# Raw query weights for every token block, a pair product on VectorE, and a new spread of the fill products in a fused attention and Fourier kernel

## The chip, the core and the metric

The kernel runs on one core of a Trainium2 chip. The metric is device time in microseconds (us) of one execution, smaller is better; it is given as the median of several runs. The engines are TensorE (PE in the profile; PEld is its weight load), VectorE (DVE), ScalarE (ACT), GpSimd (POOL) and SyncE (SP), which here issues every DMA, in its own order.

## What is computed

Two independent sublayers whose results are put side by side: multi-query attention A (32 heads of width 32, one key head and one value head) and a Fourier mixing sublayer B, on 2048 tokens of width 1024, all in float32.

```python
def _A_ref(x, wq, wk, wv, wo):                    # x: (1, 2048, 1024), wq: (1024, 1024), wk, wv: (1024, 32)
    q = (x @ wq).reshape(B, S, H, Dh).transpose(0, 2, 1, 3)
    k = x @ wk
    v = x @ wv
    scores = jnp.einsum("bhqd,bkd->bhqk", q, k) * (Dh ** -0.5)
    p = _softmax(scores, axis=-1)
    o = jnp.einsum("bhqk,bkd->bhqd", p, v)
    return o.transpose(0, 2, 1, 3).reshape(B, S, H * Dh) @ wo

def _B_ref(x, dft_seq_re, dft_seq_im, dft_hid_re, dft_hid_im):
    a = jnp.einsum("bsd,ed->bse", x, dft_hid_re)
    b = jnp.einsum("bsd,ed->bse", x, dft_hid_im)
    return jnp.einsum("ts,bse->bte", dft_seq_re, a) - jnp.einsum("ts,bse->bte", dft_seq_im, b)

return jnp.concatenate([a, b], axis=-1)
```

## The kernel before

**Two streams of matmuls, woven into one order.** Everything is written out in Python as one static program; every engine executes its instructions in the order in which they are written (the class `Ordered`, whose line 66 is therefore the line of nearly every row of the profile; tiles tell the groups apart). The first stream is attention proper. The second is the *fill*: all large matrix products (projections, both Fourier stages, the output projection), cut into *groups* that each accumulate 12 or 24 matmuls in a PSUM bank `psb`. `take(n)` writes the next n fill products; `pos["fill"]` counts them.

**Precision.** A large product of float32 matrices is made of three fast matmuls: both operands are split into a high part (a cast to float32r) and a low part (value minus high part), and `product` issues hi x hi, hi x lo and lo x hi (rows `psb<-rh,mh`, `psb<-rl,mh`, `psb<-rh,ml`). `m` are left operands (weights in `mh`, `ml`), `r` right ones (`rh`, `rl`). The cast and the subtraction are done by ACT and DVE for the first `START` = 120 products and by POOL after that (`cast`, `lo`).

**The lines that prepare operands.** `ML` handles left items, `RL` right ones. Each item passes four steps: load, combine, high part, low part. `ML` may start them 52, 36, 27 and 21 products before the item is due, and at most three raw items are staged at once (`NM0`). An item with `pre` skips load and combination: `fetch` moves its two finished parts from DRAM straight into `mh` and `ml` at the third step. An item with `save` has both parts stored to DRAM after they are made. `store` writes its DMA nine products later (`BEHIND`). `force` brings an item through all steps at once where the product needs it.

**Query groups.** `q_group(b, g, xs)` projects token block b (512 tokens, four blocks) for head group g (four heads, eight groups). Its left operand is the weight slice of head group g in two items of 256 KB. For a g that appears for the first time (block 0) they are loaded raw, split and saved in `wq_d`; in the blocks 1 to 3 the saved parts are fetched. The post step scales the result into `qh`, `ql` (parts; `ql` has one buffer) and stores both to DRAM.

**Attention.** A *unit* is a pair (b, g); there are 32 of them, with 32 steps each. `open_unit` reads a unit's query parts into the stacked operand `qst`, six steps before its scores begin. `scores(s)` makes two matmuls into `pss` (two buffers) and a negated maximum on DVE into `nm`; `row_sums` follows with the exponential on ACT and its row sums. 44 steps later (`SU + LEAD`), `expo(n)` makes the transposed scores in `pst` (one buffer) and their exponential `p`, and every eighth step `pv` multiplies by the values. Between scores and `expo` the log-sum work of the unit runs at certain steps (the table `LSE`): offsets of the two halves (`lse_1`, DVE), their exponential (`lse_1b`, ACT), the product of that with the row sums (`lse_1c`, POOL), the sum and reciprocal (`lse_2`, DVE), a transpose on PE and a copy `mt` (`lse_3`), and the DMAs that write the offsets into rows 96 and 97 of `qst` (`lse_4`). The unit's first `expo` reads these rows.

**The weave.** A prologue takes 120 products, opens unit 0, takes 66 more, and runs 44 score steps with seven products each. The main loop has 1024 steps: `score_step`, `expo`, at every eighth step `pv` and else `level(n)`, which takes as many products as bring the count to a goal that rises evenly over all steps. In the last 44 steps there are no scores left. At the end, `LAST` = 24 products are left over for the tail, and 192 products of the last block, added 12 steps before the end, follow. `aside`, called ahead of a transpose or `pv`, takes up to five products more where a group is just begun or nearly done.

Of the kernel before, what the change touches and what calls it, by code (L numbers as in the profile page):

```python
# [8 lines left out]
F32 = mybir.dt.float32  # L9
F32R = mybir.dt.float32r  # L10
AF = mybir.ActivationFunctionType
ALU = mybir.AluOpType
AX = mybir.AxisListType
# [3 lines left out]
P = 128  # L17
# [5 lines left out]
NG = 8  # L23
NQ = 4
NC = 16
# [62 lines left out]
def tile_kernel(ctx: ExitStack, tc, xT, wq, wkv, wo, xbT, wT, cT, out):  # L88
    nc = tc.nc
    te = Ordered(tc, nc.tensor)  # L90
    act = Ordered(tc, nc.scalar)
    dve = Ordered(tc, nc.vector)
    gp = Ordered(tc, nc.gpsimd)
# [3 lines left out]
    def pool(stack, name, bufs, **kw):  # L97
        kw.setdefault("reuse_waits", "tile")
        return stack.enter_context(tc.tile_pool(name=name, bufs=bufs, **kw))

    dram = ctx.enter_context(tc.tile_pool(name="dram", bufs=1, space=DRAM))
# [2 lines left out]
    oh_d = [dram.tile([NG, P, W], F32, name=f"oh_{b}") for b in range(NQ)]  # L104
    ol_d = [dram.tile([NG, P, W], F32, name=f"ol_{b}") for b in range(NQ)]
    r_d = [dram.tile([NC, P], F32, name=f"r_{u}") for u in range(NQ * NG)]
    wq_d = [[[dram.tile([P, 4, P], F32, name=f"wq_{g}_{q}_{a}") for a in range(2)] for q in range(2)] for g in range(NG)]
    xr_d = [dram.tile([P, 4, P], F32, name=f"xr_{k}") for k in range(8)]
    wr_d = [[dram.tile([P, W], F32, name=f"wr_{n}_{c}") for c in range(4)] for n in range(2)]
    u_d = {(n, k): [dram.tile([P, W], F32, name=f"{k}_{n}_{s}") for s in range(8)] for n in range(2) for k in ("t", "u2", "u3", "u4")}  # L110
# [3 lines left out]
    ident = keep.tile([P, P], F32, name="ident")  # L114
# [17 lines left out]
    op = pool(ctx, "op", 2, side="right")  # L132
    hp = pool(ctx, "hp", 1, side="right")

    def move(q, to, of):
        q.dma_start(to.bitcast(F32), of.bitcast(F32))
# [35 lines left out]
    pos = {"fill": 0, "s": 0}  # L172
# [145 lines left out]
    def store(to, of, key=None):  # L318
        def go():
            move(sp, to, of)  # L320
            if key:
                ready.add(key)
        soon(go)
# [4 lines left out]
    def bank(name, open_=False):  # L328

        b = 1 - cur["bank"] if cur["bank"] is not None else int(used[1] < used[0])  # L330
        cur["at"] += 1
        used[b] = cur["at"]
        if open_:
            cur["bank"] = b
        return ps_b[b].tile([P, W], F32, name=name)
# [16 lines left out]
    def take(n):  # L352
        for _ in range(n):
            if cur["group"] >= len(groups):
                return
            g = groups[cur["group"]]
            j = pos["fill"] - g.at
            if j == 0:
                cur["ps"] = bank("psb", True)
            if j % 3 == 0:  # L360
                RL.force(g.right[j // 3])
            if j % 12 == 0:
                ML.force(g.left[j // 12])
            product(g, cur["ps"], j)
            pos["fill"] += 1
            if j == g.n - 1:
                cur["group"] += 1
                assert all(hasattr(it, "done") for it in g.ys)
                g.post(cur["ps"])
                cur["at"] += 1  # L370
                used[cur["bank"]] = cur["at"]
                cur["bank"] = None
                if g.ys:
                    at(pos["fill"] + 2 * BEHIND, lambda n=len(g.ys): yused.__setitem__(0, yused[0] + n))
            pump()
            run_later()

    def aside():

        if cur["group"] >= len(groups):  # L380
            return
        g = groups[cur["group"]]
        j = pos["fill"] - g.at
        if 0 < j < 6:
            take(6 - j)
        elif j > g.n - 6:
            take(g.n - j)
# [29 lines left out]
        return Group(wkv_items, xs, kv_post(b), rows=2 * DH)  # L417

    ready = set()
    seen_w = set()  # L420

    def q_group(b, g, xs):
        if g in seen_w:
            left = [Item(None, pre=lambda q=q: wq_d[g][q]) for q in range(2)]
        else:
            seen_w.add(g)
            left = [Item([(lambda q=q: wq[g, :, q * 4:(q + 1) * 4, :], 1)], save=wq_d[g][q]) for q in range(2)]

        def post(ps):
            qh = op.tile([P, W], F32R, name="qh")  # L430
            ql = op.tile([P, W], F32R, name="ql", bufs=1)
            if pos["fill"] <= START:
                act.activation(qh, ps, AF.Copy, scale=scale)
            else:
                dve.tensor_scalar_mul(qh, ps, scale)
            dve.scalar_tensor_tensor(ql, ps, scale, qh.bitcast(F32), op0=ALU.mult, op1=ALU.subtract)
            store(qh_d[b][g], qh)
            store(ql_d[b][g], ql, ("q", b, g))
        return Group(left, xs, post)
# [126 lines left out]
    def x_groups(b, kv, q):  # L566
        xs = x_set(b)
        return ([kv_group(b, xs)] if kv else []) + ([q_group(b, g, xs) for g in range(NG)] if q else [])
# [12 lines left out]
    sm = pool(ctx, "sm", 2)  # L581
# [3 lines left out]
    SU = 32  # L585
    LEAD = 12
    total = SU * len(units)
    qst, nm, ls, lse, pt, ov, rb, pend = ({} for _ in range(8))
    ends = []

    def open_unit(u):
        b, g = units[u]
        assert ("q", b, g) in ready
        q = qsp.tile([P, 4, W], F32R, name="qst")
        gp.memset(q[96:P].bitcast(F32), 0.0)
        for r, src in enumerate((qh_d, ql_d, qh_d)):
            move(sp, q[r * DH:(r + 1) * DH], src[b][g].rearrange("(h d) c -> d h c", d=DH))
        qst[u] = q
        nm[u] = sm.tile([P, 6, NC], F32, name="nm")
        ls[u] = sm.tile([P, 2, NC], F32, name="ls")  # L600

    def scores(s):
        u, r = divmod(s, SU)
# [9 lines left out]
    def row_sums(s):  # L613
        if s not in pend:
            return
        ps = pend.pop(s)
        u, r = divmod(s, SU)
        i, j = divmod(r, 2)
        act.activation(ps, ps, AF.Exp, bias=nm[u][:, j, i:i + 1], accum_out=ls[u][:, j, i:i + 1])

    def over(rows):
        return rows.rearrange("p a c -> p c a")

    def lse_1(u):
        z = nm[u]
        d = sm.tile([P, 2, NC], F32, name="md")
        dve.tensor_reduce(z[:, 2], over(z[:, :2]), axis=AX.X, op=ALU.min, negate=True)
        for j in range(2):
            dve.tensor_reduce(d[:, j], over(z[:, j::2 - j][:, :2]), axis=AX.X, op=ALU.add, negate=True)
        lse[u] = d  # L630

    def lse_1b(u):
        act.activation(lse[u], lse[u], AF.Exp)

    def lse_1c(u):
        gp.tensor_mul(lse[u], lse[u], ls[u])

    def lse_2(u):
        z, d = nm[u], lse[u]
        l = sm.tile([P, NC], F32, name="l")  # L640
        dve.tensor_reduce(z[:, 3].bitcast(F32R), over(z[:, :2]), axis=AX.X, op=ALU.min)
        dve.tensor_reduce(z[:, 4], over(z[:, 2:4]), axis=AX.X, op=ALU.add, negate=True)
        dve.tensor_reduce(l, over(d), axis=AX.X, op=ALU.add)
        dve.reciprocal(z[:, 5], l)

    def lse_3(u):
        aside()
        pm = bank("psb")
        te.transpose(pm[:3 * NC, :P], nm[u][:, 3:].rearrange("p a b -> p (a b)"), ident)
        mt = sm.tile([3 * NC, P], F32, name="mt")  # L650
        dve.tensor_copy(mt, pm[:3 * NC, :P])
        cur["at"] += 1
        lse[u] = mt
# [54 lines left out]
    def score_step(s):  # L708

        if s < total:  # L710
            u, r = divmod(s, SU)
            if r == SU - 6 and u + 1 < len(units):
                open_unit(u + 1)
            scores(s)
        row_sums(s - 1)
        u, e = divmod(s - SU, SU)
        if 0 <= u < len(units):
            for f in LSE.get(e, ()):
                f(u)

    LSE = {1: (lse_1,), 2: (lse_1b,), 3: (lse_1c,), 6: (lse_2,), 7: (lse_3,), 9: (lse_4,)}

    room = [(lambda t=t, k=k: t[:, k]) for t in [pp.tile([P, 2, W], F32, name="p") for _ in range(9)] for k in range(2)]
    room += [(lambda t=t: t) for t in [hp.tile([P, W], F32, name=f"h{k}") for k in range(8)]]
# [5 lines left out]
    pump()  # L730
    take(START)
    open_unit(0)
    take(66)
    for s in range(SU + LEAD):
# [3 lines left out]
    PRO = pos["fill"]  # L738
    FILL = end[0]
    LAST = 24  # L740


    def level(n):
        k, r = divmod(n, 8)
        if r == 0:
            return
        goal = PRO + (FILL - PRO - LAST) * (k + 1) * 8 // total
        left = goal - pos["fill"]
        take(left - left * (7 - r) // (8 - r))

    for n in range(total):
        u, r = divmod(n, SU)
        if n == total - 12:
            w1 = wo_set(1)
            add([o_group(NQ - 1, t, e, ws) for e, ws in ((0, w0), (1, w1)) for t in range(4)])
        score_step(n + SU + LEAD)
        if ends:
            ends.pop(0)()
        expo(n)
        if r == 16:  # L760
            inverse(u)
        if r % 8 == 0 and n:
            pv(*divmod(n // 8 - 1, 4))
        level(n)
# [29 lines left out]
    for t, g in enumerate(last[4:]):  # L794
        ps = ps_b[t % 2].tile([P, W], F32, name="psb")
# [41 lines left out]
```

## Time and profile before

| | before |
|---|---|
| median of 3 runs | 2813.98 us (2813.29 to 2816.73) |
| the profiled execution | 2816.89 us |
| span of its trace, first to last instruction | 2815.0 us |
| mean granted TensorE clock | 0.997 |
| moved by DMA | 480.84 MB, 171 GB/s on average |

In a row of the profile, the first number of a busy entry is time in us, x is a count, and "out<-in" names the tile written and those read. In a timeline a row begins with its start and its duration; in brackets stands how long the engine had been idle before, and what ended that. The matmuls of PE are pipelined: their durations overlap, and the distance between two starts is what one costs.

### The profile page before, as it was taken

What the parts mean: (1) busy time and instruction counts of PE and PEld (TensorE: products, weight loads), DVE (VectorE), ACT (ScalarE), POOL (GpSimd) and SP (SyncE); (2) the same over time, 40 slices, a digit from 0 to 9 for tenths busy, and PEclk for the clock granted to TensorE, in tenths of its full rate; (3) what the DMA queues carried; (4) which work ended last, traced back from release to release, by engine and by line L of the source; (5) the groups of instructions that cost most, each with busy time, mean ns of one, the idle gap of its engine ahead of it and who ended that gap; (6) DMA issues with size and microseconds to landing.
All of it is one profiled execution on the core that took longest, in us unless ns stands there. A gap on an engine that the chain in (4) does not pass through costs nothing.

```text
span 2815.0 us, 40144 instructions
## 1 busy us (share of the span) xinstructions
PE 2776.0 (99%) x13904; PEld 1935.7 (69%) x13904; DVE 1612.9 (57%) x1800; ACT 2182.6 (78%) x3151; POOL 1569.4 (56%) x1558
## 2 busy tenths in 40 slices
PE   7999999999999999999999999989999999999999
PEld 5776676767667676767666767666767676766656
DVE  5766666666666665555555555545555555555411
ACT  4578887888878788888888888878888888888740
POOL 2422233665545448767785676887888875721110
PEclk9999999999999999999999999999999999999999
DMA  8865435675576555554463454564554642545345
GB/s 292 299 199 163 156 109 169 225 231 188 195 243 211 166 178 167 152 155 142 140 191 105 127 172 122 184 198 138 183 176 146 187 139 98 159 145 145 122 143 172
DMA packets 315723, 480.84 MB, mean 171 GB/s; under 512 B 33408, under 2 KB 98432, under 8 KB 315520
## 3 DMA queue, kind: packets, MB, share of 16 engines
q1 hardware_dynamic: 315520, 478.28, 54.3%
q8 instruction: 110, 1.80, 0.3%
q14 instruction: 93, 0.76, 0.1%
HBM read 364.12 MB, written 112.98 MB: 169 GB/s over the span
## 4 chain that ended last, share of the span: by engine, by line
PE 93%; DMA 2%; POOL 1%; issue 1%; DVE 1%; SPq 1%; ACT 1%; POOLq 0%; DVEq 0%; ACTq 0%
PE psb L66 59%; PE pss L66 18%; PE pst L66 17%; DMA r<-s 1%; DMA ql<-ql 1%; SPq L66 1%; POOL ml L66 0%; DMA r<-in_xT_dram 0%; DVE nm L66 0%; POOL mh L66 0%; POOL m L66 0%; DMA wq<-mh 0%; POOL rl L66 0%; POOL rh L66 0%; POOL y L66 0%
## 5 line engine op out<-in xcount | busy, mean ns | idle before, releaser
L66 DVE TENSOR_REDUCE nm<-pss 128x1 f32<-128x1024 f32 x1024 | 1252.2, 1223 | 611.7 <-PE pss L66 610.9
L66 ACT ACTIVATE p<-pst 128x1024 f32<-128x1024 f32 x1024 | 1052.0, 1027 | 481.0 <-PE pst L66 478.9
L66 ACT ACTIVATE pss<-pss,nm 128x1024 f32<-128x1024 f32 x1024 | 1112.7, 1087 | 72.7 <-DVE nm L66 71.6
L66 PE MATMUL psb<-rh,mh 128*128 128x512 f32 (+1 forms) x1852 | 732.0, 395 | 17.9 <-ACT rh L66 8.7
L66 PE MATMUL psb<-rh,ml 128*128 128x512 f32 (+1 forms) x1852 | 731.9, 395 | 1.4 <-POOL ml L66 1.4
L66 PE MATMUL psb<-rl,mh 128*128 128x512 f32 (+1 forms) x1852 | 730.1, 394 | 0.3 <-DVE rl L66 0.3
L66 PE MATMUL pst<-qst,kst 128*128 128x512 f32 x2048 | 654.3, 400 | 5.6 <-DMA qst<-mt 4.7
L66 PE MATMUL pss<-kst,qst 128*128 128x512 f32 x2048 | 655.8, 401 | 3.2 <-ACT pss L66 3.2
L66 PEld LDWEIGHTS pss<-kst,qst 128*128 128x128 f32 x2048 | 375.6, 188 | 185.3 <-issue 100.5
L66 PE MATMUL psb<-p,v 128*32 128x512 f32 x4096 | 466.6, 596 | 0.0
L66 PEld LDWEIGHTS pst<-qst,kst 128*128 128x128 f32 x2048 | 375.8, 188 | 116.6 <-ACT p L66 26.6
L66 PEld LDWEIGHTS psb<-rh,mh 128*128 128x128 f32 (+1 forms) x1852 | 347.6, 188 | 105.8 <-ACT rh L66 10.0
L66 PEld LDWEIGHTS psb<-rh,ml 128*128 128x128 f32 (+1 forms) x1852 | 347.8, 188 | 86.0 <-POOL ml L66 2.8
L66 PEld LDWEIGHTS psb<-rl,mh 128*128 128x128 f32 (+1 forms) x1852 | 347.4, 188 | 84.2 <-DVE rl L66 1.4
L66 POOL TENSOR_TENSOR ml<-m,mh 128x512 fp32r<-128x512 f32 x292 | 376.5, 1289 | 49.2 <-ACT mh L66 43.6
L66 PEld LDWEIGHTS psb<-p,v 128*32 128x32 f32 x4096 | 120.5, 110 | 276.3 <-issue 266.0
L66 POOL TENSOR_TENSOR r<-r,r 128x512 f32<-128x512 f32 x112 | 144.3, 1288 | 269.7 <-DMA r<-in_wT_dram 135.0
L66 POOL CAST rh<-r 128x512 fp32r<-128x512 f32 x214 | 131.2, 613 | 275.0 <-PE psb L66 110.1
L66 POOL TENSOR_TENSOR rl<-r,rh 128x512 fp32r<-128x512 f32 x214 | 276.0, 1290 | 5.5
L66 POOL TENSOR_TENSOR m<-m,m 128x512 f32<-128x512 f32 x192 | 247.6, 1290 | 24.4 <-DMA m<-in_xbT_dram 18.8
L66 DVE TENSOR_TENSOR ov<-ov,psb 128x512 f32<-128x512 f32 x96 | 66.0, 687 | 314.2 <-PE psb L66 314.2
L66 POOL CAST mh<-m 128x512 fp32r<-128x512 f32 x291 | 178.0, 612 | 91.4 <-PE psb L66 76.0
(69 smaller groups left out, 926.5 us busy)
## 6 DMA issues: line engine op xcount, KB each, us to landing
m<-in_cT_dram SPq DMA_DIRECT2D x384, 256.0 KB, 3.8
r<-s SPq DMA_DIRECT2D x192, 256.0 KB, 4.4
y<-y SPq DMA_DIRECT2D x96, 256.0 KB, 4.6
r<-in_wT_dram SPq DMA_DIRECT2D x80, 256.0 KB, 3.6
m<-in_xbT_dram SPq DMA_DIRECT2D x80, 256.0 KB, 4.2
y<-u SPq DMA_DIRECT2D x80, 256.0 KB, 2.9
qst<-qh SPq DMA_DIRECT2D x64, 256.0 KB, 5.7
s<-y SPq DMA_DIRECT2D x64, 256.0 KB, 2.9
```

Source lines behind the costliest of these rows:

```text
L66: return lambda *a, **k: self.tc.keep_in_program_order(f(*a, **k))
```

## The change

Three edits. (1) No query weight part is kept in DRAM: `wq_d` is gone, and each of the four token blocks loads each weight item raw and splits it. (2) The product of the exponentiated offsets with the row sums moves from POOL (`lse_1c`) to DVE, as two reductions with a multiplication in `lse_2`; for that, the row sums and offsets become rows 6 to 9 of `nm`, and the table `LSE` has the steps 1, 2, 4, 6, 8 in place of 1, 2, 3, 6, 7, 9. (3) The goal of `level` no longer rises evenly: each step past `QUIET` = 980 has one product more, and all steps share the rest.

```diff
--- before.py
+++ after.py
@@ -104,7 +104,6 @@
     oh_d = [dram.tile([NG, P, W], F32, name=f"oh_{b}") for b in range(NQ)]
     ol_d = [dram.tile([NG, P, W], F32, name=f"ol_{b}") for b in range(NQ)]
     r_d = [dram.tile([NC, P], F32, name=f"r_{u}") for u in range(NQ * NG)]
-    wq_d = [[[dram.tile([P, 4, P], F32, name=f"wq_{g}_{q}_{a}") for a in range(2)] for q in range(2)] for g in range(NG)]
     xr_d = [dram.tile([P, 4, P], F32, name=f"xr_{k}") for k in range(8)]
     wr_d = [[dram.tile([P, W], F32, name=f"wr_{n}_{c}") for c in range(4)] for n in range(2)]
     u_d = {(n, k): [dram.tile([P, W], F32, name=f"{k}_{n}_{s}") for s in range(8)] for n in range(2) for k in ("t", "u2", "u3", "u4")}
@@ -417,14 +416,9 @@
         return Group(wkv_items, xs, kv_post(b), rows=2 * DH)
 
     ready = set()
-    seen_w = set()
 
     def q_group(b, g, xs):
-        if g in seen_w:
-            left = [Item(None, pre=lambda q=q: wq_d[g][q]) for q in range(2)]
-        else:
-            seen_w.add(g)
-            left = [Item([(lambda q=q: wq[g, :, q * 4:(q + 1) * 4, :], 1)], save=wq_d[g][q]) for q in range(2)]
+        left = [Item([(lambda q=q: wq[g, :, q * 4:(q + 1) * 4, :], 1)]) for q in range(2)]
 
         def post(ps):
             qh = op.tile([P, W], F32R, name="qh")
@@ -585,7 +579,7 @@
     SU = 32
     LEAD = 12
     total = SU * len(units)
-    qst, nm, ls, lse, pt, ov, rb, pend = ({} for _ in range(8))
+    qst, nm, lse, pt, ov, rb, pend = ({} for _ in range(7))
     ends = []
 
     def open_unit(u):
@@ -596,8 +590,7 @@
         for r, src in enumerate((qh_d, ql_d, qh_d)):
             move(sp, q[r * DH:(r + 1) * DH], src[b][g].rearrange("(h d) c -> d h c", d=DH))
         qst[u] = q
-        nm[u] = sm.tile([P, 6, NC], F32, name="nm")
-        ls[u] = sm.tile([P, 2, NC], F32, name="ls")
+        nm[u] = sm.tile([P, 10, NC], F32, name="nm")
 
     def scores(s):
         u, r = divmod(s, SU)
@@ -616,28 +609,26 @@
         ps = pend.pop(s)
         u, r = divmod(s, SU)
         i, j = divmod(r, 2)
-        act.activation(ps, ps, AF.Exp, bias=nm[u][:, j, i:i + 1], accum_out=ls[u][:, j, i:i + 1])
+        act.activation(ps, ps, AF.Exp, bias=nm[u][:, j, i:i + 1], accum_out=nm[u][:, 8 + j, i:i + 1])
 
     def over(rows):
         return rows.rearrange("p a c -> p c a")
 
     def lse_1(u):
         z = nm[u]
-        d = sm.tile([P, 2, NC], F32, name="md")
         dve.tensor_reduce(z[:, 2], over(z[:, :2]), axis=AX.X, op=ALU.min, negate=True)
         for j in range(2):
-            dve.tensor_reduce(d[:, j], over(z[:, j::2 - j][:, :2]), axis=AX.X, op=ALU.add, negate=True)
-        lse[u] = d
+            dve.tensor_reduce(z[:, 6 + j], over(z[:, j::2 - j][:, :2]), axis=AX.X, op=ALU.add, negate=True)
 
     def lse_1b(u):
-        act.activation(lse[u], lse[u], AF.Exp)
-
-    def lse_1c(u):
-        gp.tensor_mul(lse[u], lse[u], ls[u])
+        act.activation(nm[u][:, 6:8], nm[u][:, 6:8], AF.Exp)
 
     def lse_2(u):
-        z, d = nm[u], lse[u]
+        z = nm[u]
+        d = sm.tile([P, 2, NC], F32, name="md")
         l = sm.tile([P, NC], F32, name="l")
+        for j in range(2):
+            dve.tensor_reduce(d[:, j], over(z[:, 6 + j::2][:, :2]), axis=AX.X, op=ALU.mult)
         dve.tensor_reduce(z[:, 3].bitcast(F32R), over(z[:, :2]), axis=AX.X, op=ALU.min)
         dve.tensor_reduce(z[:, 4], over(z[:, 2:4]), axis=AX.X, op=ALU.add, negate=True)
         dve.tensor_reduce(l, over(d), axis=AX.X, op=ALU.add)
@@ -646,7 +637,7 @@
     def lse_3(u):
         aside()
         pm = bank("psb")
-        te.transpose(pm[:3 * NC, :P], nm[u][:, 3:].rearrange("p a b -> p (a b)"), ident)
+        te.transpose(pm[:3 * NC, :P], nm[u][:, 3:6].rearrange("p a b -> p (a b)"), ident)
         mt = sm.tile([3 * NC, P], F32, name="mt")
         dve.tensor_copy(mt, pm[:3 * NC, :P])
         cur["at"] += 1
@@ -718,7 +709,7 @@
             for f in LSE.get(e, ()):
                 f(u)
 
-    LSE = {1: (lse_1,), 2: (lse_1b,), 3: (lse_1c,), 6: (lse_2,), 7: (lse_3,), 9: (lse_4,)}
+    LSE = {1: (lse_1,), 2: (lse_1b,), 4: (lse_2,), 6: (lse_3,), 8: (lse_4,)}
 
     room = [(lambda t=t, k=k: t[:, k]) for t in [pp.tile([P, 2, W], F32, name="p") for _ in range(9)] for k in range(2)]
     room += [(lambda t=t: t) for t in [hp.tile([P, W], F32, name=f"h{k}") for k in range(8)]]
@@ -740,12 +731,18 @@
     LAST = 24
 
 
+    QUIET = total - SU - LEAD
+    MORE = 1
+
+    def goal(n):
+        return PRO + (FILL - PRO - LAST - MORE * (total - QUIET)) * n // total + MORE * max(n - QUIET, 0)
+
+
     def level(n):
         k, r = divmod(n, 8)
         if r == 0:
             return
-        goal = PRO + (FILL - PRO - LAST) * (k + 1) * 8 // total
-        left = goal - pos["fill"]
+        left = goal((k + 1) * 8) - pos["fill"]
         take(left - left * (7 - r) // (8 - r))
 
     for n in range(total):
```

## The prediction

> **What bounds the kernel now.** I read the page first: which engine is full, and whether its clock is whole.
>
> ```profile
> PE 2776.0 (99%) x13904; PEld 1935.7 (69%) x13904; DVE 1612.9 (57%) x1800; ACT 2182.6 (78%) x3151; POOL 1569.4 (56%) x1558
> PE 93%; DMA 2%; POOL 1%; issue 1%; DVE 1%; SPq 1%; ACT 1%; POOLq 0%; DVEq 0%; ACTq 0%
> ```
>
> TensorE (PE) is occupied 2776.0 of 2815.0 us and is 93% of the chain that ended last. The diff neither adds nor removes a matmul, so time can come only from three places: the 39 us in which PE stands, stretches in which it is busy but slow, and stretches in which another engine dictates the step while PE's occupied time hides it. Next I read the table by stretches for where the first kind lies.
>
> ```profile
> 60.00:80.00 20.00, 15.15 (x50) 11.17 (x51) 7.68 (x8) 4.81 (x8) 15.84 (x19) 0.83 1.04 386
> 80.00:100.00 20.00, 20.00 (x88) 16.21 (x87) 15.00 (x17) 11.84 (x19) 11.39 (x12) 1.00 0.89 310
> 300.00:400.00 100.00, 100.00 (x513) 69.62 (x512) 63.57 (x75) 82.62 (x121) 31.27 (x34) 1.00 0.41 128
> 2720.00:2740.00 20.00, 19.93 (x106) 11.51 (x109) 2.07 (x3) 9.26 (x10) 6.49 (x8) 1.00 0.48 142
> ```
>
> Columns: stretch, length, busy time of PE, weight loads, DVE, ACT, POOL, then granted clock, DMA share, GB/s. From 60 to 80 us PE loses 4.85 us, the granted clock is 0.83, and the DMA engines are full (share 1.04). From 80 on PE is gapless, with POOL at 11.39 of 20 us. At 2720 the page shows a full PE; the instructions below show otherwise.
>
> **Part A: the weight parts no longer stored.** I followed PE's timeline through the bad stretch. "psb" matmuls are fill products, "pss" the first scores.
>
> ```profile
> 54.25 0.47 PE L66 MATMUL psb<-rh,mh 128*128 128x512 f32 x1
> 57.57 0.40 PE L66 MATMUL psb<-rh,ml 128*128 128x512 f32 x1
> 60.40 0.50 PE L66 MATMUL psb<-rh,mh 128*128 128x512 f32 x1 [2.43 <-POOL mh L66]
> 62.34 0.63 PE L66 MATMUL psb<-rh,mh 128*128 128x512 f32 x1
> 62.77 0.63 PE L66 MATMUL psb<-rl,mh 128*128 128x512 f32 x1
> 63.62 0.90 PE L66 MATMUL pss<-kst,qst 128*128 128x512 f32 x2
> 66.72 0.47 PE L66 MATMUL psb<-rh,mh 128*128 128x512 f32 x1 [0.82 <-DVE ql L66]
> 74.54 1.22 PE L66 MATMUL pss<-kst,qst 128*128 128x512 f32 x2 [3.18 <-ACT pss L66]
> 80.33 0.62 PE L66 MATMUL pss<-kst,qst 128*128 128x512 f32 x2
> ...
> 80.95 1.62 PE psb L66 x7
> 83.04 1.62 PE psb L66 x7
> ```
>
> The last two lines are of the chain of waits: seven products take 1.62 us, 0.2317 us each, and a prologue step of seven products and two score matmuls takes 83.04 - 80.95 = 2.09 us. The product at 54.25 is number 168 (seven groups of 24). Scores begin after number 186, and the pair at 80.33 is the sixth, five steps later. Unhindered that is 18 x 0.2317 + 5 x 2.09 = 14.6 us; it took 26.08. So 11.5 us are lost here. The waits shown are 6.4 of them. After each long wait the products also start 0.43 apart (62.34, 62.77) instead of 0.23.
>
> [...]
>
> Who is late? DMA issues from 50 to 80 us, SP's and POOL's queues, and DVE's:
>
> ```profile
> DMA packets 5695, 10.38 MB, mean 346 GB/s; under 512 B 633, under 2 KB 633, under 8 KB 5694
> m<-in_wq_dram SPq DMA_DIRECT2D x9, 256.0 KB, 5.1
> wq<-mh SPq DMA_DIRECT2D x8, 256.0 KB, 5.2
> wq<-ml SPq DMA_DIRECT2D x8, 256.0 KB, 5.2
> ...
> 47.93 0.39 SPq L66 DMA_DIRECT2D ql<-ql  x1
> 52.72 0.32 SPq L66 DMA_DIRECT2D qst<-qh  x1
> 54.21 0.38 SPq L66 DMA_DIRECT2D m<-in_wq_dram  x1
> ...
> 59.74 0.61 POOL L66 CAST mh<-m 128x512 fp32r<-128x512 f32 x1 [4.40 <-DMA m<-in_wq_dram]
> 65.88 0.69 DVE L66 SCALAR_TENSOR_TENSOR ql<-psb,qh 128x512 fp32r<-128x512 f32 x1 [10.91 <-DMA ql<-ql]
> ```
>
> Two chains. The load issued at 54.21 lands only at 59.74, so POOL's cast and PE are late. And ql has one buffer: its next writer on DVE waits 10.91 us for the previous store, with the score reductions behind it on DVE, and so the exponentials (ACT) and the score banks PE waits for (3.18). In both the DMA engines are full, and 16 transfers of 256 KB, 4.2 of the stretch's 10.4 MB, are the wq stores that the change deletes. Each also takes SP about half a microsecond of issue. One delay stays: SP stands from 48.3 to 52.72 for the first query store to land, as the load of qst must follow it. With the traffic down to 60% I expect landing nearer 3 us than 5, the load issued at 52 and landed at 56, just ahead of its need at 57.8. Bounds: nothing (the traffic was not the cause) to 11.5. I take 8.5, near the upper end since both chains end in a transfer that shared full DMA engines.
>
> **Part B: raw weights in blocks 1 to 3.** 96 fetches of parts (2 per item) become 48 raw loads, and POOL gains 48 casts and 48 subtractions:
>
> ```profile
> L66 POOL TENSOR_TENSOR ml<-m,mh 128x512 fp32r<-128x512 f32 x292 | 376.5, 1289 | 49.2 <-ACT mh L66 43.6 <-PE psb L66 1.7
> L66 POOL CAST mh<-m 128x512 fp32r<-128x512 f32 x291 | 178.0, 612 | 91.4 <-PE psb L66 76.0 <-DMA m<-in_xbT_dram 8.7 <-DMA m<-in_wq_dram 5.3
> L66 POOL TENSOR_TENSOR md<-md,ls 128x32 f32<-128x32 f32 x32 | 8.1, 253 | 160.8 <-ACT md L66 160.0 <-PE psb L66 0.8
> L66 DVE TENSOR_REDUCE md<-nm 128x16 f32<-128x32 f32 x64 | 9.0, 183 | 1.1
> ```
>
> 48 x (1.289 + 0.612) = 91 us of POOL. A group needs two weight items and about one item of the next x set, 3 x 1.9 = 5.7 us. It lasts 24/7 steps of 2.09, 7.2 us, in the prologue; in the main loop, with 4.84 products a step (part D), 24/4.84 steps of at least 2.09, over 10.4 us. So POOL is at 80%, then below 55%; in block 0 it carries that load already and PE is gapless from 80 to 100. Parts are made 21 products ahead, and DMA at 0.41 has room. Cost: nothing, hidden under PE's products; if the cover fails, part A's wait comes back (a rival below).
>
> **Part C: the pair product.** POOL loses 32 products of 253 ns; DVE gains 64 reductions, priced by the nearest row at 183 ns: 11.7 us, in DVE's 43% idle time. What matters is the order. Now DVE's sum waits in order for POOL, the reductions and a bank's release behind it. With two ACT and DVE instructions instead, the exponential was issued two steps earlier, ahead of the exponentials that free the score bank DVE reads just before. So no new wait. The transpose comes two steps behind its input instead of one, and the move of the offsets into qst one step earlier (8, not 9). The worst unit:
>
> ```profile
> 1857.03 0.19 DVE L66 TENSOR_REDUCE l<-md 128x16 f32<-128x32 f32 x1 [2.12 <-POOL md L66]
> 1858.50 0.67 DVE L66 TENSOR_TENSOR h<-h,psb 128x512 f32<-128x512 f32 x1
> ...
> 1857.56 0.29 PE L66 MATMUL psb<-ident,nm 128*48 128x128 f32 x1 [1.66 <-DVE nm L66]
> 1859.32 0.51 PE L66 MATMUL psb<-rh,mh 128*128 128x512 f32 x1 [1.00 <-POOL r L66]
> 1876.03 1.19 PE L66 MATMUL pst<-qst,kst 128*128 128x512 f32 x2 [4.72 <-DMA qst<-mt]
> ...
> 1869.83 0.81 SPq L66 DMA_DIRECT2D m<-in_cT_dram  x2
> 1871.69 1.71 SPq L66 DMA_DIRECT2D qst<-mt  x2
> ```
>
> POOL late, so DVE late, so the transpose (1.66) and the bank that h's addition empties (1.00; the page names POOL, but this fits). Then qst's move stands in SP's queue behind loads until 1871.69. 7.4 us of waits, and slow products after them. The first 2.7 should go; of the 4.72, an earlier issue by one step (over 2 us) should save most, about 3; slow products 0.8 more. I take 6.5. Bounds: -2 (SP's order changes, and another unit's move is late by a step) to 9 (all waits with their slow products).
>
> **Part D: one more product in the last 44 steps.** Now every main step takes (5472 - 497 - 24)/1024 = 4.84 products: the groups before the final eight hold 36 x 24 + 112 x 12 + 112 x 24 + 24 x 24 = 5472, the prologue uses 120 + 66 + 44 x 7 and about 3 that close a group, and 24 are kept for last. So 44 x 980/1024 = 42 products leave the first 980 steps, where PE sets the pace: 42 x 0.2317 = 9.7 us saved. They reappear at the end:
>
> ```profile
> 2710.55 0.73 PE L66 MATMUL pst<-qst,kst 128*128 128x512 f32 x2
> 2712.46 0.73 PE L66 MATMUL pst<-qst,kst 128*128 128x512 f32 x2
> 2709.47 1.03 ACT L66 ACTIVATE p<-pst 128x1024 f32<-128x1024 f32 x1 [0.88 <-PE pst L66]
> ```
>
> Scores are over here, and each step is a ring through the single pst buffer: matmul, 1.03 us of exponential, matmul. It takes 1.91 us with five products (2710.55 to 2712.46), although these seven matmuls need only 7 x 0.2317 = 1.62. A sixth product makes 1.85 and is free; a seventh makes 9 x 0.2317 = 2.09, so costs 0.18. Following the goal formula through these steps gives about 13 steps with seven (2.3 us), and five more products beside the p,v matmuls (1.1). Net 9.7 - 3.4 = 6.3 us. Bounds: 0 (the first 980 steps gain nothing, ACT setting them) to 9.7.
>
> **Sum.** 8.5 + 0 + 6.5 + 6.3 = 21.3 us. The profiled execution took 2816.9 us, the runs' median is 2814.0. By the one the new time is 2795.6, by the other 2792.7. I predict midway, 2794, that is 2815.4 less the gain.
>
> **Rivals.** (1) *The waits move.* SP's stand for the first query store is still there and its load still late, so A gives 4; in stage 2 POOL, near full, makes another qst move late, so C gives 0. 2815.4 - 10.3 = 2805. For it: SP's 4.4 us stand. Against: a third of the traffic is gone. (2) *Everything recovered*: A 11.5, C 9, D 7.5: 28 us, 2787. Against: SP's stand at 48.3 us remains. (3) *Slower: raw loads of blocks 1 to 3 come late*, because SP, which waits for POOL to free staging buffers, issues them behind other waits. The pattern is that of 60.40: the six products from 57.8 should have ended at 59.2, the score came at 63.62, so 4.4 us per miss. From five misses of 48 it eats the gain; with eight, 2815.4 - 21.3 + 35.2 = 2829. For: block 0 had such a miss in its 14 items. Against: DMA at 0.41 and POOL at 31.27 of 100 us there. (4) *Nothing comes of it*: a burst of loads replaces the stores, A 4, and ACT, whose two exponentials fill a five-product step, limits the first 980 steps, C and D 0: 2811.
>
> **How the numbers follow.** Forecast 0.60, with its own range 2788 to 2801; rivals in order 0.18, 0.10, 0.07, 0.05. A measurement here can tell about 0.2%, 5.6 us, from no change. The forecast, (1) and (2) are faster by more: 0.88; (4) is the same: 0.05; (3) slower: 0.07. The range runs from 2785 (below rival 2) to 2809 (past rival 1); it leaves out (3) and (4), and some edge.
>
> **What would show it.** Right: no PE wait over 1 us from 50 to 80, clock 1.00 and DMA well under 0.9 there, the sixth score pair near 72 us; POOL some 80 us busier, all before 360; no wait for md or qst<-mt over 1 us near 1860; the first 980 main steps about 1 us shorter per 100, and the last 44 filled with six or seven products at 1.91 to 2.09. Wrong: PE waits for POOL mh between 100 and 360 us, or the stretch from the first main step to the last score shortens by less than 5 us beyond the waits named.

## The result and the profile after

| | before | after |
|---|---|---|
| median | 2813.87 us (2813.29 to 2816.73, 4 runs) | 2797.23 us (2795.68 to 2801.67, 4 runs) |
| the profiled execution, and its span | 2816.89, 2815.0 us | 2797.06, 2795.1 us |

The ratio of after to before is 0.9941, 95% interval 0.9924 to 0.9959: 16.6 us faster by the medians, 19.8 by the profiled executions. To see where, I cut both traces at the starts of ACT's exponentials of the transposed scores (`p<-pst`, one per main step): the first one, the 981st, the last.

| stretch | before, us | after, us | difference | predicted |
|---|---|---|---|---|
| start to first main step | 164.74 | 156.08 | -8.66 | -8.5 (A) |
| first 980 main steps | 2494.81 | 2480.24 | -14.57 | -9.7 (D) and -6.5 (C) |
| the last steps, to the 1024th | 94.65 | 97.94 | +3.29 | +3.4 (D) |
| tail | 60.8 | 60.8 | 0 | 0 |

The page's engine line and the table by stretches of the changed kernel (columns as before):

```profile
PE 2764.2 (99%) x13904; PEld 1931.4 (69%) x13904; DVE 1621.7 (58%) x1864; ACT 2181.3 (78%) x3151; POOL 1650.5 (59%) x1622
...
40.00:60.00 20.00, 20.00 (x91) 16.27 (x90) 6.87 (x11) 2.38 (x4) 13.52 (x15) 1.00 0.81 259
60.00:80.00 20.00, 18.42 (x81) 14.62 (x80) 14.04 (x16) 10.50 (x17) 15.34 (x18) 1.00 0.66 222
80.00:100.00 20.00, 20.00 (x87) 16.06 (x86) 14.90 (x16) 11.14 (x20) 15.74 (x18) 1.00 0.46 154
300.00:400.00 100.00, 100.00 (x511) 68.94 (x510) 62.29 (x72) 82.84 (x121) 36.45 (x38) 1.00 0.34 109
```

From 60 to 80 us the DMA share fell from 1.04 to 0.66, the clock is whole, and PE loses 1.6 us where it lost 4.85. POOL is 81 us busier in all, and PE is gapless from 80 to 100 and from 300 to 400 as before.

The start in SP's queue and on PE, then the bad unit near 1850 us on PE, DVE and SP:

```profile
44.83 0.32 SPq L66 DMA_DIRECT2D ql<-ql  x1
46.84 0.32 SPq L66 DMA_DIRECT2D qst<-qh  x1
48.74 0.35 SPq L66 DMA_DIRECT2D m<-in_wq_dram  x1
...
66.23 0.73 PE L66 MATMUL pss<-kst,qst 128*128 128x512 f32 x2 [1.58 <-ACT pss L66]
70.49 0.62 PE L66 MATMUL pss<-kst,qst 128*128 128x512 f32 x2
142.83 0.47 PE L66 MATMUL psb<-rh,mh 128*128 128x512 f32 x1 [1.69 <-DVE ql L66]
1855.61 0.70 PE L66 MATMUL pst<-qst,kst 128*128 128x512 f32 x2 [3.56 <-DMA qst<-mt]
...
1839.91 0.27 DVE L66 COPY mt<-psb 48x128 f32<-48x128 f32 x1
...
1848.74 0.81 SPq L66 DMA_DIRECT2D m<-in_cT_dram  x2
1850.60 1.15 SPq L66 DMA_DIRECT2D qst<-mt  x2
```

SP's stand for the first query store shrank from 4.4 us to 1.7 (45.15 to 46.84), and the sixth score pair comes at 70.49 in place of 80.33. In the bad unit (unit 20, counted from 0) the wait for the pair product is gone, but `mt` is ready at 1840.2 and its move is issued only at 1850.60, behind loads; the loads themselves came late, at 1842.76 and 1848.74, right behind POOL's subtractions `ml<-m,mh`, which ended at 1842.73 and 1848.71. PE stands 3.56 us where it stood 4.72.

Of the last steps, three rows with a distance of one step each, and two from further on, all from PE's timeline:

```profile
2665.55 0.74 PE L66 MATMUL pst<-qst,kst 128*128 128x512 f32 x2
2667.73 0.62 PE L66 MATMUL pst<-qst,kst 128*128 128x512 f32 x2
2669.82 0.62 PE L66 MATMUL pst<-qst,kst 128*128 128x512 f32 x2
...
2692.45 0.67 PE L66 MATMUL pst<-qst,kst 128*128 128x512 f32 x2
2694.35 0.67 PE L66 MATMUL pst<-qst,kst 128*128 128x512 f32 x2
```

The first of these steps takes 2.18 us, the second 2.09, both with seven products; the third, with six, takes 1.90. Of the last 44 steps 13 have seven, as forecast.

### The profile page after: what moved, and what is told of

It reads as the page before. It is cut to its first block, busy times and chain, and to the rows that moved or that the text cites. A ratio compares the mean times of both kernels' runs of the same rounds, so it can differ in the third digit from the quotient of the medians.

```text
span 2795.1 us, 40153 instructions
## 1 busy us (share of the span) xinstructions
PE 2764.2 (99%) x13904; PEld 1931.4 (69%) x13904; DVE 1621.7 (58%) x1864; ACT 2181.3 (78%) x3151; POOL 1650.5 (59%) x1622
## 4 chain that ended last, share of the span: by engine, by line
PE 93%; DMA 2%; POOL 1%; issue 1%; DVE 1%; ACT 1%; SPq 1%; POOLq 0%; ACTq 0%; DVEq 0%
PE psb L66 59%; PE pss L66 18%; PE pst L66 16%; DMA r<-s 1%; SPq L66 1%; POOL ml L66 0%; DMA p<-in_xT_dram 0%; DVE nm L66 0%; DMA r<-in_xT_dram 0%; ACT pss L66 0%; DVE y L66 0%; ACT p L66 0%; POOL mh L66 0%; ACT rh L66 0%; DMA ql<-ql 0%
## 5 line engine op out<-in xcount | busy, mean ns | idle before, releaser
L66 POOL TENSOR_TENSOR ml<-m,mh 128x512 fp32r<-128x512 f32 x340 | 438.7, 1290 | 48.3 <-ACT mh L66 40.6
L66 POOL CAST mh<-m 128x512 fp32r<-128x512 f32 x339 | 207.4, 612 | 169.0 <-PE psb L66 149.8
```

Source lines behind the costliest of these rows:

```text
L66: return lambda *a, **k: self.tc.keep_in_program_order(f(*a, **k))
```

## The experiments

Open were whether the parts add up, whether the stores cause the loss at the start, whether VectorE or the earlier places helped in part C, and why the wait for `qst<-mt` stayed. The table has, for each profiled execution, the time to the first main step, the first 980 main steps, the rest to the 1024th, and the lengths of unit 15 and unit 20 (32 steps each, counted from 0, from a unit's first exponential to the next unit's); then the median and the ratio to before, with its interval, from runs of before on the same chip beside it. The changed kernel was timed apart from the others: the median of before was 2813.87 us beside it, and 2814.83 to 2815.21 beside them, so differences of medians between its row and another hold to about 1.3 us.

| run | start | first 980 | last | unit 15 | unit 20 | median | ratio (95%) |
|---|---|---|---|---|---|---|---|
| before | 164.74 | 2494.81 | 94.65 | 81.95 | 90.85 | 2813.87 | |
| after | 156.08 | 2480.24 | 97.94 | 80.51 | 86.09 | 2797.23 | 0.9941 (0.9924, 0.9959) |
| spread_only | 163.92 | 2487.66 | 98.50 | 86.13 | 87.91 | 2814.42 | 0.9996 (0.9988, 1.0005) |
| raw_only | 154.87 | 2492.71 | 94.66 | 80.60 | 89.78 | 2806.90 | 0.9969 (0.9957, 0.9981) |
| pair_only | 166.64 | 2486.47 | 94.63 | 80.58 | 82.50 | 2808.97 | 0.9977 (0.9968, 0.9986) |
| after_stores | 166.09 | 2480.85 | 97.96 | 80.52 | 87.43 | 2808.38 | 0.9974 (0.9964, 0.9985) |
| raw_pair | 156.06 | 2484.69 | 94.70 | 80.58 | 81.93 | 2801.61 | 0.9951 (0.9937, 0.9964) |
| late_lse | 158.05 | 2493.69 | 98.46 | 86.44 | 87.91 | 2810.27 | 0.9985 (0.9977, 0.9994) |
| pool_early | 158.26 | 2481.81 | 97.95 | 80.83 | 88.59 | 2800.64 | 0.9953 (0.9940, 0.9965) |
| mt_act | 157.96 | 2535.98 | 97.94 | 85.49 | 95.76 | 2854.57 | 1.0144 (1.0130, 1.0158) |
| more2 | 156.09 | 2468.55 | 105.26 | 80.06 | 84.36 | 2799.43 | 0.9944 (0.9931, 0.9956) |
| ql_y | 154.09 | 2478.95 | 97.90 | 80.52 | 86.76 | 2796.70 | 0.9941 (0.9927, 0.9954) |
| early_lse | 156.47 | 2477.04 | 98.79 | 80.88 | 82.82 | 2793.75 | 0.9923 (0.9911, 0.9936) |
| early_ql | 153.26 | 2475.86 | 98.78 | 80.84 | 82.49 | 2789.84 | 0.9910 (0.9897, 0.9924) |

**The three parts alone.** `spread_only` is the kernel before with the new `goal` alone.

> The kernel before with only the new goal of the fill products. Theory (the sum by parts): the first 980 main steps lose 42 products of 0.2317 us, about 9.7 us, and the last 44 steps grow by about 3.3, so 6 to 6.5 us faster than before, ratio near 0.9977; the start and the wait near 1870 us stay. Rival (ACT limits the first 980 steps): these steps do not get shorter, so 3 us slower.

By the medians it gives nothing that can be measured, against the 6 to 6.5 us expected. The rival's cause falls all the same, as the first 980 steps are 7.15 us shorter. The trace says where most of the gain went: the last steps cost 3.85 us more as expected, all units but 15 and 20 together are 8.4 us shorter (7.15, plus 4.18 lost in unit 15, less 2.94 gained in unit 20), but unit 15, undisturbed before, has a new stall:

```profile
1460.47 1.19 PE L66 MATMUL pst<-qst,kst 128*128 128x512 f32 x2 [4.20 <-DMA qst<-mt]
...
1449.72 0.33 SPq L66 DMA_DIRECT2D m<-in_cT_dram  x1
1455.28 0.33 SPq L66 DMA_DIRECT2D m<-in_cT_dram  x1
1456.66 1.15 SPq L66 DMA_DIRECT2D qst<-mt  x2
```

Moving products shifts the weave's phase against the units, and with it where SP's loads stand ahead of the small move: here the move is issued 10.0 us after `mt` is ready, behind two loads that had waited for POOL. The 8.4 us come near 42 times 0.23; that the saving stays was wrong.

`raw_only` is the kernel before with the raw loads alone (the three lines of `q_group` and no `wq_d`).

> The kernel before with only the raw weight loads. Theory: the time to the first main step falls from 164.7 to about 156 us and nothing else moves, so 8.7 us faster, ratio near 0.9969. Rival (the raw loads and POOL's 91 us in blocks 1 to 3 cost time later): the main steps grow by over 2 us and the gain is under 6.5.

The start is 9.9 us shorter, the main steps did not grow: 2.1 us shorter, 1.35 and 1.07 of it in the units 15 and 20, and no other differs by over 0.15. POOL's 91 us cost nothing that shows. The theory holds.

`pair_only` is the kernel before with the new log-sum work alone.

> The kernel before with only the pair product on VectorE and the earlier steps of the log-sum work. Theory: the wait for the pair product in the worst unit (2.7 us) goes, the late move into qst stays or shrinks a little, so the main steps are 3 to 5 us shorter, ratio 0.998 to 0.999. Rival (the unit's stall has another cause, such as the weave's phase, and the gain there came from the moved fill products): under 1.5 us, or none.

```profile
1868.18 0.70 PE L66 MATMUL pst<-qst,kst 128*128 128x512 f32 x2 [1.26 <-DMA qst<-mt]
```

Its main steps are 8.3 us shorter, more than the theory's 3 to 5, and all of it in unit 20 (90.85 to 82.50); the gains and losses of the others cancel. The wait for the move, 4.72 us before, is 1.26 here. The rival falls.

By the ratios the three parts alone save 0.31%, 0.23% and 0.04%, in sum 0.58% or 16.3 us; together they save 0.59%, 16.6 us. So they add up, as far as intervals of about 0.1% on each can tell.

**The stores.** `after_stores` is the changed kernel that also stores block 0's parts, which nothing reads (the line that makes `wq_d`, as before, is left out here):

```diff
-        left = [Item([(lambda q=q: wq[g, :, q * 4:(q + 1) * 4, :], 1)]) for q in range(2)]
+        left = [Item([(lambda q=q: wq[g, :, q * 4:(q + 1) * 4, :], 1)], save=wq_d[g][q] if b == 0 else None) for q in range(2)]
```

> The changed kernel, which also stores the weight parts of block 0 to DRAM as before did, and never reads them. Theory (the stores fill the DMA engines and SP's queue at the start): the first main step comes 8 to 9 us later, near 165 us, and the whole is 8 to 9 us slower than the changed kernel. Rival (the gain came from the later blocks, which no longer fetch parts): under 3 us slower.

```profile
59.66 0.50 PE L66 MATMUL psb<-rh,mh 128*128 128x512 f32 x1 [1.49 <-POOL mh L66]
66.36 0.47 PE L66 MATMUL psb<-rh,mh 128*128 128x512 f32 x1 [0.89 <-DVE ql L66]
74.92 1.22 PE L66 MATMUL pss<-kst,qst 128*128 128x512 f32 x2 [3.91 <-ACT pss L66]
```

The three waits of before are back at their places, though of other lengths, the start is 10.0 us longer, the main steps are the changed kernel's to 0.6 us. The stores alone made the loss; the fetches of the later blocks made none.

**The spread in company.** `raw_pair` is the changed kernel with `MORE = 0`, `more2` with `MORE = 2`.

> The changed kernel with the old, even goal of the fill products. Theory (42 products of 0.2317 us leave the first 980 steps, and stalls that depend on the weave's phase take part of it back): the last 44 steps are 3.3 us shorter than the changed kernel's 97.9, the first 980 are 6 to 10 us longer, of which units other than 20 carry 9 to 10 and unit 20 itself gets shorter; 3 to 6 us slower in all. Rival (the spread is worth nothing here either, as alone): within 1.5 us.

The first 980 steps are 4.45 us longer, and 8.6 without unit 20, which is itself 4.2 shorter; the last steps are 3.2 shorter. The sizes come near the theory's (8.6 where 9 to 10 stood, 3.2 where 3.3 stood), but the first 980 steps as a whole stay under its 6 to 10. By the trace the spread is worth 1.2 us, which is the rival's case; by the medians 4.4, which is the theory's; the profiled execution is the lowest of its five, and the two intervals overlap. So what the spread is worth in company stays open between 1 and 4 us.

> The changed kernel with two more fill products per step in the last 44 steps in place of one. Theory (the sixth product is free there, the seventh costs 0.18 us, the eighth its full 0.23): the first 980 steps are 9.7 us shorter but for stalls that move, the last 44 longer by 8 to 10, so within 2 us of the changed kernel. Rival (the last steps have more room than the ring of 1.91 us shows): 4 us or more faster.

First steps 11.7 us shorter, last ones 7.3 longer, where 9.7 and 8 to 10 were expected. By the traces that is 4.4 us faster, as the rival had it, but this profiled execution, 2792.83 us, is the lowest of five by 4.9; by the medians the kernel is 2.2 us slower, and the ratio is that of the changed kernel. So no gain is shown. In the ring, a step with eight products takes 2.31 us for 2.09 with seven: the room is used up, as expected.

**Engine or place.** `late_lse` is the changed kernel with the pair product on VectorE, but the old places; `pool_early` has the new places, but the product on POOL. The edit of `late_lse`:

```diff
-    LSE = {1: (lse_1,), 2: (lse_1b,), 4: (lse_2,), 6: (lse_3,), 8: (lse_4,)}
+    LSE = {1: (lse_1,), 2: (lse_1b,), 6: (lse_2,), 7: (lse_3,), 9: (lse_4,)}
```

> The changed kernel with the pair product on VectorE, but with the log-sum steps at the places of before (sum at 6, transpose at 7, moves at 9). Theory A (the engine is what helped, the places little): the wait for DVE nm ahead of a transpose stays gone, and unit 20 is within 1.5 us of the changed kernel's 86.1. Theory B (the earlier issue of the moves is what helped): the wait for qst<-mt grows by about 2 us, and a wait of over 1 us comes up in some other unit of the second Fourier stage, 2 to 5 us slower in all.

13 us slower by the medians, and in the trace the first 980 steps are 13.45 us longer. Theory A falls: unit 20 is 1.8 us longer than the changed kernel's. Theory B is right in kind, as another unit has a wait of 4.54 us for the move, but not in size, and the wait in unit 20 did not grow (3.34 us). The grouped rows of the transpose's weight load, before, after, and here with the wait:

```profile
L66 PEld LDWEIGHTS psb<-ident,nm 128*48 128x48 f32 x32 | 3.3, 103 | 11.0 <-DVE nm L66 6.9 <-DVE ql L66 1.5 <-DVE y L66 0.9
```

```profile
L66 PEld LDWEIGHTS psb<-ident,nm 128*48 128x48 f32 x32 | 3.3, 102 | 1.4
```

```profile
L66 PEld LDWEIGHTS psb<-ident,nm 128*48 128x48 f32 x32 | 3.3, 102 | 12.7 <-DVE nm L66 8.8 <-DVE y L66 1.3 <-DVE ql L66 1.1
...
1456.82 1.19 PE L66 MATMUL pst<-qst,kst 128*128 128x512 f32 x2 [4.54 <-DMA qst<-mt]
```

The first figure behind the last bar is the idle time ahead of that load: 11.0 us, then 1.4, then 12.7. With the sums on DVE only one step ahead of the transpose, the weight load stands about a third of a microsecond per unit. But this idle time alone costs nothing that shows: `pair_only` also has 1.4, and its units other than 15 and 20 are together 1.4 us longer than before's; `early_lse` below has 13.8, and is faster than the changed kernel.

```profile
L66 PEld LDWEIGHTS psb<-ident,nm 128*48 128x48 f32 x32 | 3.3, 102 | 13.8 <-DVE ov L66 13.4
```

The stall of unit 15 makes 5.9 of the 13.45, unit 20 grows by 1.8, and 5.7 us are spread over the others. `spread_only`, with the old places and the product on POOL, has the stall of unit 15 too, while its other units, 15 and 20 aside, are together as long as the changed kernel's. So the stall belongs to the later moves, and the 5.7 us to VectorE's reductions at the old places, by a way that no run shows.

> The changed kernel with its new places of the log-sum work (sum at 4, transpose at 6, moves at 8) but the pair product on POOL again, at step 3. Theory (the places help, and VectorE is what allows them, since POOL comes late to the product in the second Fourier stage): the sum on DVE waits for POOL there, waits of PE for DVE nm over 1 us come back near 1850 us, 2 to 8 us slower than the changed kernel. Rival (only the places count): main steps within 1.5 us of the changed kernel's 2480.2, as two small DVE instructions per unit are saved.

```profile
1844.86 0.19 DVE L66 TENSOR_REDUCE l<-md 128x16 f32<-128x32 f32 x1 [8.65 <-POOL md L66]
```

```profile
1845.94 0.29 PE L66 MATMUL psb<-ident,nm 128*48 128x128 f32 x1 [4.29 <-DVE ov L66]
```

DVE waits 8.65 us for POOL's late product, PE 4.29 for DVE, as the theory had it; but the first 980 steps grow by only 1.6 us, a hair over the rival's 1.5, as the wait for `qst<-mt` is gone in turn. By the medians it is 3.4 us slower, with overlapping intervals, and 2.2 of the trace's 3.8 lie in the start, which varies by about that. So the places carry part C; VectorE adds 1.6 us to it in the first 980 steps, and at the old places it costs: these steps of `late_lse` are 6.0 us longer than those of `spread_only`, which otherwise differs from it only in the weight loads.

**Why the move into qst is late.** `mt_act` issues the two moves from ACT's queue (`move(act, ...)` for `move(sp, ...)` in `lse_4`).

> The changed kernel, but the two small moves of the offsets into qst are issued from ACT's queue in place of SP's. Theory (the wait of 3.56 us at 1855.6 us is the place of these moves in SP's queue, behind loads that wait for POOL): no wait for qst<-mt over 0.5 us is left in any unit, unit 20 (86.1 us) comes down to 81 to 82.5, and the whole is 3 to 5 us faster than the changed kernel, less 64 issues on ACT that PE's products hide. Rival (POOL is late as a whole in that stretch, and PE would stand for its operands anyway): the wait becomes one for POOL ml, unit 20 stays above 84.5, under 1.5 us gained.

Neither case came. ACT's instructions and issues in one unit, and between them SP's next issue:

```profile
1361.17 0.52 ACTq L66 DMA_DIRECT2D qst<-mt  x1
1364.15 0.81 SPq L66 DMA_DIRECT2D m<-in_cT_dram  x2
...
1367.21 0.52 ACTq L66 DMA_DIRECT2D qst<-mt  x1
1367.78 1.02 ACT L66 ACTIVATE p<-pst 128x1024 f32<-128x1024 f32 x1 [5.59 <-DMA m<-in_cT_dram]
```

The second issue stood for about 5 us, and the exponentials behind it on ACT with it: 56 us lost in the main steps, 55.3 of them in the seven units with such a stand. The trace says why one queue's issue waits for another's load. A transfer reports its landing on a semaphore (a counter that an engine can wait for, raised 16 times per transfer in the trace of after); this program's queues share eight of them in turn, and in all 1936 cases of the trace, as in all 1936 of after's, an issue came only after the transfer that had its semaphore before had landed. The second issue's is number 106, which the load that SP issued at 1364.15 had; that load landed at 1367.19. All eight stands of 2.8 us or more end so, 0.02 to 0.03 us after a transfer of SP's. The move left SP's queue, but not the wait for what SP issues late. So this run does not tell the theories apart. `early_lse` does, by giving SP more lead:

```diff
-    LSE = {1: (lse_1,), 2: (lse_1b,), 4: (lse_2,), 6: (lse_3,), 8: (lse_4,)}
+    LSE = {1: (lse_1,), 2: (lse_1b,), 3: (lse_2,), 5: (lse_3,), 7: (lse_4,)}
```

> The changed kernel with sum, transpose and moves one step earlier again (3, 5, 7). Theory (the wait of 3.56 us near 1855 us is the place of the two moves in SP's queue, behind loads): two more microseconds of lead take that wait below 1.5 us or away, unit 20 (86.1) comes to 81 to 84, 2 to 5 us faster than the changed kernel. Rival (the sum now comes too early for ACT's exponential, or the transpose for the sum): PE waits for DVE nm in most units, 3 us slower or more.

```profile
1844.01 1.25 SPq L66 DMA_DIRECT2D qst<-mt  x1
1847.73 0.82 SPq L66 DMA_DIRECT2D m<-in_cT_dram  x2
...
1828.65 0.50 PE L66 MATMUL psb<-rh,ml 128*128 128x512 f32 x1 [1.59 <-POOL ml L66]
1870.32 0.50 PE L66 MATMUL psb<-rh,ml 128*128 128x512 f32 x1 [2.79 <-POOL ml L66]
```

The move is now issued ahead of the loads, no wait for `qst<-mt` of 0.2 us or more is left in any unit, and unit 20 is 3.3 us shorter. POOL's own lateness shows next, 2.79 us in unit 21, which is 2.1 us longer for it. So the place in SP's queue made the wait, but of its end only 1.2 us stay over the two units, as `mt_act`'s rival had it; the rest of the gain, 3.2 us in the first 980 steps, lies in other units. The ratio falls to 0.9923, 3.5 us below the changed kernel by the medians, with intervals that overlap.

**The other buffer.** `ql_y` gives `ql` the six buffers of the pool `yp`.

```diff
-            ql = op.tile([P, W], F32R, name="ql", bufs=1)
+            ql = yp.tile([P, W], F32, name="y0").bitcast(F32R)
```

> The changed kernel, but the low part of the queries has six buffers (those that the Fourier stages' accumulators use later) in place of one. Theory (the waits that are left at 66.2 and 142.8 us, 1.58 and 1.69, come from the one buffer of ql, whose store must land): both go, the first main step comes 3 to 4 us earlier, near 152.5. Rival (the score bank waits for ACT in any case): under 1 us.

```profile
140.84 0.47 PE L66 MATMUL psb<-rh,mh 128*128 128x512 f32 x1 [1.69 <-DVE y L66]
...
140.01 0.69 DVE L66 SCALAR_TENSOR_TENSOR y<-psb,qh 128x512 fp32r<-128x512 f32 x1
```

Half right: the wait at 66.2 is gone and the start 2.0 us shorter; the other stays to the hundredth, now under the buffer's new name, so it was no store's landing but DVE still reading the bank (until 140.70). With both, `early_ql`:

> As the last, and with the low part of the queries in six buffers in place of one, which took the first main step from 156.1 to 154.1 us by itself. Theory: both gains add, 4 to 7 us faster than the changed kernel, ratio to before near 0.992. Rival: stalls move with the phase, and it is within 2 us of it.

Both gains add: 2789.84 us, 25.4 below before and 7.4 below the changed kernel by the medians, a little more than the 4 to 7 expected, and its interval (0.9897 to 0.9924) touches the changed kernel's only at its upper end. The rival falls.

## Why the prediction was right, point by point

The median came at 2797.2 for 2794 forecast, inside the likeliest case's own range, and the mechanism was mostly the one described. The gain was 16.6 us by the medians where 21.3 were summed up, and the term that fell short is D.

- **A, 8.5 us for the stores:** 8.66 between the two traces, 7.9 by the medians of `raw_only`. Both chains were as told, and `after_stores` brings them back. That the trace agrees to 0.2 us is luck, as the start of kernels that do not differ there varies by 3 us: it is 154.9 to 158.3 us in the eight runs without the stores and with the old buffer, 163.9 to 166.6 in the four with them; the means lie 8.6 apart. The load after SP's stand was issued at 48.74, earlier than the 52 allowed for, since the stand too shrank; it took 4.2 us to land, not nearer 3.
- **B, nothing for POOL's extra work:** right, as `raw_only` shows. POOL is 90.6 us busier up to 360 us, near the 91 summed up, and 9.5 less after that. Rival 3 had no miss at all in 48 items.
- **C, 6.5 us:** alone, the ratio 0.9977 (0.9968 to 0.9986) makes 6.5 us, 3.9 to 9.0, and the trace 8.3. "An earlier issue by one step should save most, about 3" of the 4.72 was right for the part alone, where it saved 3.5 (`pair_only`), but not with the spread, where it saved 1.2: with the phase moved, SP's loads stood ahead of the move again.
- **D, 6.3 us net:** the last steps, 3.3 for 3.4, and the other units' saving, 8.4 to 8.6 for 9.7, were near. The term that failed is "42 x 0.2317 = 9.7 us saved" as a sum that stays: a shift of the phase cost 4.2 us in unit 15 alone (`spread_only`) and 4.2 in unit 20 in company (`raw_pair`). Left are 3.3 us alone and 1.2 in company by the traces, 1.1 us (-1.4 to 3.4) alone by the ratio. Stalls that move stood only in part C's bound and in rival 1, not in this term.
- **Two signs that did not come:** PE still waited over 1 us in the start (1.58 at 66.23) and for `qst<-mt` in unit 20 (3.56). The first was the single buffer of `ql`, as `ql_y` shows, the second the move's place behind late loads, as `early_lse` shows.
- **The base:** the profiled execution of before lay 2.9 us above the median, and midway was a guess; it put the forecast 1.4 us nearer to the result than the median of before would have. The gain by the profiled executions, 19.8, is nearer to the sum of 21.3 than the 16.6 of the medians.

## What to carry to other kernels

Where one engine is full, look for a ring beside it whose own pace leaves room: a sixth product was free in steps where PE showed as busy (1.90 us with six after, 1.91 with five before). Idle time of a weight load is a place to look, not yet a gain: in `pair_only` 9.6 of its 11.0 us went, and outside the two units that stalled nothing was gained. Save an intermediate to DRAM only where the store's time slot has room; here, reading and splitting the weights again cost nothing that shows (main steps 2.1 us shorter in `raw_only`), storing them about 9 us (8.6 between the means of the starts). And in a hand-woven order, moving work by a few products re-deals which small transfer stands behind which load, so cure the late transfer (more lead) before counting small gains.

## What the hardware showed that was not expected

**Slow matmuls after a wait.** Behind PE's waits of 1.58 and 1.69 us the products start 0.23 us apart, behind 2.43 (before) and 3.56 us (after) soon 0.42 to 0.43. The length of the wait does not decide it alone, though: behind 3.15 us in `ql_y`, the last three rows, they stay 0.23 apart.

```profile
66.80 0.40 PE L66 MATMUL psb<-rh,mh 128*128 128x512 f32 x1
67.03 0.39 PE L66 MATMUL psb<-rl,mh 128*128 128x512 f32 x1
...
1856.40 0.63 PE L66 MATMUL psb<-rl,mh 128*128 128x512 f32 x1
1856.82 0.63 PE L66 MATMUL psb<-rh,ml 128*128 128x512 f32 x1
...
1854.22 0.70 PE L66 MATMUL pst<-qst,kst 128*128 128x512 f32 x2 [3.15 <-DMA qst<-mt]
1854.75 0.39 PE L66 MATMUL psb<-rh,mh 128*128 128x512 f32 x1
1854.98 0.39 PE L66 MATMUL psb<-rl,mh 128*128 128x512 f32 x1
```

The granted clock shows where the slow products lie. In the trace of before it is at 0.50 for 3.41 us from 60.80, 74.46 and 1859.63 us each and for 6.83 from 1873.28, in that of after for 3.41 from 1856.35, and whole elsewhere up to PE's last product. The four starts in before lie 13.65, 1785.17 and 13.65 us apart, 4, 523 and 4 times 3.413 us. I divided both traces into stretches of 3.413 us that fall in with these starts, from 14 us on. Five stretches at whole clock come right ahead of one at half: in them PE stood 3.10, 2.43, 2.34 and 1.97 us in sum (before) and 2.67 us (after). In all others at whole clock it stood less, at most 1.75 (before) and 1.69 us (after), and whole clock followed. The 2.43 us of before lie in one such stretch, from 57.39 to 60.80. How the 3.15 us of `ql_y` lie, and so why no slow products follow them, is not shown. So the prediction's slow products behind 2.43 us were read rightly, but not every wait of that length brings them.

**A DMA issue on a busy engine's queue.** The 57 us lost in `mt_act` are not the price of 64 issues of 8 KB: in units without a stand, all but two differ from the changed kernel's by less than 0.6 us. They are the price of what an issue waits for, here the landing of a transfer from another queue.
